# Convolution of every fifth block moved from TensorE to GpSimd, and the stores from GpSimd to SyncE

## The chip, the cores and the metric

One Trainium2 chip, one core. The metric is the time of one execution on the device in microseconds. Times of a kernel are medians of several runs; spans in the profile are 1.7 to 3.0 us shorter than the run they were taken in, in the median 1.8. A ratio is the mean time of one kernel's fast runs over that of the other's of the same rounds, so it is not quite the ratio of the medians quoted. Medians and ranges are over all runs, ratios over the fast ones alone; only e8 and e11 have a run that is labelled slow, one each.

## The reference

```python
# x: (8, 4160, 192), weight: (8 heads, 7 taps); w1, w2, w3: (192, 768), w_out: (768, 192)
w = exp(weight - max); w = w / (sum(w) + 1e-9)               # per head
out[b, s, h, :] = sum_k w[h, k] * x_pad[b, s + k, h, :]      # causal, 6 zeros ahead, 24 columns a head
h = maximum(maximum(out @ w1, out @ w2), out @ w3)           # 33280 tokens
result = h @ w_out                                           # fp32
```

## The kernel before

The tokens are cut into 65 blocks of 512. For 61 of them (four at the start have another form) the convolution goes: load x, cast it to fp16 on GpSimd, multiply it on TensorE with a band matrix that holds the seven taps (tile G, one group of 16 matmuls for a pair of blocks), copy G out of PSUM on ScalarE and VectorE, transpose the result by DMA, and copy it to the other half of the partitions ("double"). Then come six steps a block of the first layer (tiles lp and lq), a maximum (h), and the second layer (po).

```python
def cast_x(t):                                    # GpSimd, twice a block
    ...
    for c in range(2):
        nc.gpsimd.tensor_copy(out=x16s[t0][0:K, :, c, u, :, :].rearrange("p h r c -> p r h c"),
                              in_=xf[0:K, c:NR:2, :].rearrange("p r (h c) -> p r h c", c=GRP))

def conv(t, pools):                               # TensorE, once for two blocks
    ...
    for h in range(NHEAD):
        for c in range(2):
            nc.tensor.matmul(G[h // per][HALF * c:HALF * (c + 1), h % per, :],
                lhsT=band[0:HALF + PAD, h, PAD:HALF + PAD],
                rhs=x16s[t0][0:HALF + PAD, h, c, :, :, :].rearrange("p u r c -> p (u r c)"), ...)

for t in range(2, NB):                            # the main loop (cut)
    load_x(t + 6)                                 # SyncE
    double(t + 2)                                 # SyncE, two DMAs
    cast_x(t + 5)                                 # GpSimd
    l1(t, 0)
    conv(t + 3 if t % 2 == 0 else NB, WW + PQ); evac(...)
    turn(t + 3)                                   # SyncE, DMA transpose
    st2(t - 1, 0, NJ)
    for j in range(1, NJ):
        l1(t, j); st2(t - 1, j, NJ)
    store(t - 1, 0, 4, (nc.gpsimd,))              # GpSimd
```

In the traces GpSimd, and SyncE too, works through its instructions in this order.

The softmax here doesn't subtract the row's maximum and nothing guards it: scores larger than these inputs give would overflow.

## Time and profile before

| | before |
|---|---|
| median of 4 runs | 468.05 us (467.33 to 471.71) |
| span of the profiled run | 466.3 us |
| TensorE busy | 99% |
| GpSimd busy | 35% |
| VectorE, ScalarE busy | 77%, 68% |

The lines themselves stand in the prediction below. In a line of groups the columns are source line, engine, operation, output and inputs, shapes and count; then busy time in us and the mean ns of one; then the idle time of the engine just ahead of them and what ended it.

### The profile page before, as it was taken

The numbers are of one execution on the slowest core, as the hardware profiler recorded it, in microseconds if no ns is written. First come the engines' busy times: TensorE is split into PE (matmuls) and PEld (weight loads), VectorE is DVE, ScalarE is ACT, GpSimd is POOL, SyncE is SP. The second block draws the span as 40 slices with busy tenths as digits, with TensorE's granted clock in tenths as the row PEclk, the third lists the DMA queues.
The fourth block names the chain that finished last, engine by engine and source line by source line (L and its number), as shares of the span: only waits on it lengthen the run. The fifth ranks groups of instructions, "written<-read, shape, count | busy, mean of one in ns | idle before, by whom it ended". The sixth has DMA issues, their size and how long they took to land.

```text
span 466.3 us, 17191 instructions
## 1 busy us (share of the span) xinstructions
PE 460.1 (99%) x7065; PEld 385.6 (83%) x7065; DVE 359.6 (77%) x607; ACT 317.0 (68%) x609; POOL 162.7 (35%) x227
## 2 busy tenths in 40 slices
PE   8899999999999999999999999999999999999996
PEld 4587888888888888889888888988888898888996
DVE  6787777777777777787877777777778777787775
ACT  5766767667666676676766667676676666766664
POOL 5664334234324324423423432432442343243010
PEclk9999999999999999999999999999999999999999
DMA  8958997778687777878777768767686976784512
GB/s 201 238 119 198 208 232 174 171 198 172 170 202 191 149 188 174 180 175 204 178 152 197 170 181 189 181 157 200 177 176 165 210 178 153 190 166 108 118 69 103
DMA packets 107114, 81.14 MB, mean 174 GB/s; under 512 B 53110, under 2 KB 101980, under 8 KB 107036
## 3 DMA queue, kind: packets, MB, share of 16 engines
q1 hardware_dynamic: 99804, 55.17, 57.6%
q0 software_dynamic: 7072, 24.78, 14.8%
q8 instruction: 55, 0.90, 0.9%
q14 instruction: 23, 0.19, 0.1%
q10 hardware_dynamic: 160, 0.10, 0.1%
HBM read 30.28 MB, written 25.56 MB: 120 GB/s over the span
## 4 chain that ended last, share of the span: by engine, by line
PE 95%; DMA 2%; SPq 2%; POOL 0%; issue 0%; DVE 0%; ACT 0%
PE lq L399 34%; PE po L442 33%; PE lp L399 22%; PE G L301 5%; DMA wos<-in_moe_w_out_dram 2%; SPq L190 1%; PE D L319 0%; SPq L134 0%; POOL wo L515 0%; PE pm L280 0%; PE pm L284 0%; DVE o L452 0%; ACT a L451 0%
## 5 line engine op out<-in xcount | busy, mean ns | idle before, releaser
L404 DVE TENSOR_TENSOR h<-r,lq 128x512 f16<-128x512 f16 x386 | 264.5, 685 | 98.6 <-ACT r L403 98.6
L403 ACT ACTIVATE r<-lp 128x512 f16<-128x512 f32 x386 | 230.5, 597 | 137.4 <-PE lp L399 123.9
L399 PE MATMUL lp<-yd,wd 64*128 64x512 f16 x1158 | 311.9, 376 | 1.3 <-DVE wd L256 1.3
L399 PE MATMUL lq<-yd,wd 64*128 64x512 f16 x1158 | 312.0, 376 | 0.0
L442 PE MATMUL po<-wo,h 64*128 64x192 f16 x3120 | 248.9, 243 | 0.0
L442 PEld LDWEIGHTS <-h 64*128 64x128 f16 x3120 | 203.6, 94 | 17.4
L399 PEld LDWEIGHTS <-wd 64*128 64x128 f16 x2340 | 166.6, 94 | 28.0 <-issue 3.4
L471 POOL DMA_DIRECT2D out_dram<-o x64 | 48.1, 752 | 281.4 <-DVE o L452 215.0
L158 POOL CAST x<-xf 70x768 f16<-70x768 f32 x122 | 97.4, 833 | 3.0 <-DMA xf<-in_x_dram 2.6
L442 PE MATMUL po<-m,yd 64*128 64x192 f16 x780 | 95.7, 243 | 0.0
L452 DVE TENSOR_TENSOR o<-a,po 128x384 f32<-128x384 f32 (+1 forms) x132 | 71.3, 542 | 0.6 <-ACT a L451 0.6
L442 PEld LDWEIGHTS <-yd 64*128 64x128 f16 x780 | 57.8, 94 | 10.8
L451 ACT COPY a<-po 128x384 f32<-128x384 f32 (+1 forms) x132 | 62.0, 471 | 2.1 <-PE po L442 2.1
L347 DVE CAST ys<-G 128x384 f16<-128x384 f32 x61 | 31.0, 550 | 0.0
L301 PEld LDWEIGHTS <-band 70*64 70x64 f16 x496 | 19.5, 109 | 12.8 <-PE lp L399 12.7
L347 ACT CAST ys<-G 128x384 f16<-128x384 f32 x61 | 26.2, 485 | 0.0
L301 PE MATMUL G<-x,band 70*64 70x192 f16 (+1 forms) x496 | 26.1, 248 | 0.0
L215 PE MATMUL idle<-idle 128*128 128x512 f16 x15 | 6.5, 581 | 1.2 <-DVE idle L210 1.2
L177 POOL CAST xz<-xf 112x80 f16<-112x80 f32 (+2 forms) x18 | 5.4, 340 | 3.9 <-DMA xf<-in_x_dram 3.0
L319 PEld LDWEIGHTS <-xz 112*32 112x32 f16 x240 | 4.7, 107 | 2.0 <-issue 1.3
L319 PE MATMUL D<-band,xz 112*32 112x103 f16 (+1 forms) x240 | 5.5, 229 | 0.0
L335 DVE COPY yd<-yd 64x512 f16<-64x512 f16 x9 | 4.3, 474 | 1.0 <-ACT yd L328 0.5
(45 smaller groups left out, 51.3 us busy)
## 6 DMA issues: line engine op xcount, KB each, us to landing
xf<-in_x_dram SPq DMA_DIRECT2D x57, 420.0 KB
out_dram<-o POOLq DMA_DIRECT2D x62, 384.0 KB, 3.8
yd<-yd SPq DMA_DIRECT2D x122, 96.0 KB
xf<-in_x_dram SPq DMA_DIRECT2D x7, 367.5 KB
ws<-in_moe_w_dram SPq DMA_DIRECT2D x6, 192.0 KB
yd<-ys SPq DMA_TRANSPOSE x61
w3s<-in_moe_w_dram SPq DMA_DIRECT2D x3, 192.0 KB
wos<-in_moe_w_out_dram SPq DMA_DIRECT2D x1, 576.0 KB
```

Source lines behind the costliest of these rows:

```text
L158: nc.gpsimd.tensor_copy(out=x16s[t0][0:K, :, c, u, :, :].rearrange("p h r c -> p r h c"), in_=xf[0:K, c:NR:2, :].rearrange("p r (h c) -> p ...
L215: nc.tensor.matmul(ps[:], lhsT=idle[:, 0:P], rhs=idle[:], start=True, stop=True)
L301: nc.tensor.matmul(G[h // per][HALF * c:HALF * (c + 1), h % per, :], lhsT=band[0:HALF + PAD, h, PAD:HALF + PAD], rhs=x16s[t0][0:HALF + PAD ...
L319: nc.tensor.matmul(ps[32 * g:32 * g + 32, lo:hi], lhsT=xz[t][v][0:rlen, q, 32 * s:32 * s + 32], rhs=band[0:rlen, h, cc:cc + hi - lo], star ...
L347: copy(out=slots[t][:, :, :, GRP * per * i:GRP * per * (i + 1)].rearrange("p u r (h c) -> p h (u r) c", c=GRP), in_=G[i][:].rearrange("p h ...
L399: nc.tensor.matmul(ps[i][:, 0:N], lhsT=wd[row, c, P * j:P * (j + 1)], rhs=y_all(t, i, c), start=(c == 0), stop=(c == NC - 1))
L403: nc.scalar.activation(out=r[:, 0:N], in_=ps[0][:, 0:N], func=AF.Relu)
L404: nc.vector.tensor_max(out=hs[t][:, j, 0:N], in0=r[:, 0:N], in1=ps[1][:, 0:N])
L442: nc.tensor.matmul(ps[b0, i][:, s % 2, :], lhsT=a, rhs=b, start=first, stop=last)
L451: nc.scalar.copy(out=a[:, ss, :], in_=ps[s0, 0][:, ss, :])
L452: nc.vector.tensor_add(out=outs[t][:, s0:s + 1, :], in0=a[:, ss, :], in1=ps[s0, 1][:, ss, :])
L471: qs[0].dma_start(out=bass.AP(tensor=out.tensor, offset=r * D, ap=[[D, n], [step * D, s1 - s0], [1, D]]), in_=ob[p0:p0 + n, s0:s1, :])
```

## The change

Its intent: TensorE is the bound and GpSimd is mostly idle, so twelve blocks (positions 11, 16, ... 61 and 64, called moved blocks here) get their convolution on GpSimd. x is cast and transposed first, so that tokens lie along the free dimension; then a tap is a multiplication by a column of weights and an addition in fp32. The six tokens ahead of a stretch of 128 come from its neighbour by two small DMAs and a copy (the "lead"). To make room on GpSimd, SyncE issues the stores. The blocks also change places, so that each moved block but the first of a sequence has its neighbour in the moved block before it.

```diff
+    EVERY = 5
+    qpos = [q for q in range(11, NB - 3, EVERY)] + [NB - 1]
 ...
+    def lead_q(q):
+        ... # memset if the block starts a sequence, else a DMA from the previous moved block
+        nc.sync.dma_start(out=xt[HALF:P, 0:6:2, LEAD - PAD:LEAD], in_=xt[0:HALF, 1:6:2, T - PAD:T])
+        nc.gpsimd.tensor_copy(out=xt[:, 1:6:2, LEAD - PAD:LEAD], in_=xt[:, 0:6:2, T - PAD:T])
+    def tap_q(q, k):
+        for c in range(3):
+            nc.gpsimd.tensor_scalar(out=part[:, 2 * c:2 * c + 2, :], in0=xt[...shifted by k...],
+                                    scalar1=wcol[:, c, k:k + 1], scalar2=0.0, op0=mult, op1=add)
+        ... nc.gpsimd.tensor_add(out=accs[q][:], in0=accs[q][:], in1=part[:])
 ...
+    for n, q in enumerate(qpos):
+        w = min(4 + EVERY * n, NB - 7)
+        plan.setdefault(w - 5 if n else 2, {})["load"] = q
+        plan.setdefault(w - 2 if n else 3, {})["cast"] = q
+        plan.setdefault(w - 1 if n else 4, {})["turn"] = q
+        plan.setdefault(w, {})["lead"] = q
+        for k in range(KW):
+            plan.setdefault(w + (k // 2 if last else k * EVERY // KW), {}).setdefault("taps", []).append((q, k))
+    make_wcol()
     for t in range(2, NB):
         load_x, double ...
+        if "turn" in todo: turn_q(todo["turn"])
+        if "lead" in todo: lead_q(todo["lead"])
         cast_x(t + 5)
+        if "load" in todo: load_q(todo["load"])
         l1, conv, evac, turn ...
+        if "cast" in todo: cast_q(todo["cast"])
+        for q, k in todo.get("taps", ()): tap_q(q, k)
         st2, l1 ...
-            store(t - 1, 0, 4, (nc.gpsimd,))
+            store(t - 1, 0, 4, (nc.sync,))
```

Iteration w of a moved block is thus the one in which its lead is fetched and its first two taps are computed; the transpose is issued in iteration w - 1 (for the first moved block in w itself).

More of the change, by code (lines that the diff above doesn't have):

```diff
@@ L69 @@
     NB = len(blocks)
+    EVERY = 5
+    qpos = [q for q in range(11, NB - 3, EVERY)] + [NB - 1]
+    qset = set(qpos)
     ENDS = NB - 7
-    blocks.insert(ENDS, blocks.pop())
+    ends = blocks.pop()
+    lanes = blocks[-nfull:] + blocks[-2 * nfull:-nfull]
+    lanes, rest = lanes[:len(qpos)], [blk for blk in blocks if blk not in lanes[:len(qpos)]]
+    rest.insert(ENDS - sum(q < ENDS for q in qpos), ends)
+    blocks = [(lanes if t in qset else rest).pop(0) for t in range(NB)]
     blkN = [sum(sg[2] for sg in blk) for blk in blocks]
@@ L98 @@
     xfp = ctx.enter_context(tc.tile_pool(name="xfp", bufs=6))
+    xqp = ctx.enter_context(tc.tile_pool(name="xqp", bufs=2))
+    xtp = ctx.enter_context(tc.tile_pool(name="xtp", bufs=3))
+    accp = ctx.enter_context(tc.tile_pool(name="accp", bufs=2))
     x16p = ctx.enter_context(tc.tile_pool(name="x16p", bufs=3))
@@ L113, in load_x @@
     def load_x(t, eng=nc.sync):
-        if not 0 <= t < NB:
+        if not 0 <= t < NB or t in qset:
             return
@@ L140, in load_x @@
         xin[t] = [xf, todo[0][0], parts]
+    pairs, left = {}, [t for t in range(NDENSE + 1, NB) if t not in qset]
+    assert len(left) % 2 == 0
+    for a in left[::2]:
+        b = left[left.index(a) + 1]
+        assert b == a + 1
+        pairs[a], pairs[b] = (a, 0, 2), (a, 1, 2)
+    pairs[NDENSE] = (NDENSE, 0, 1)
     def place(t):
-        return (t, 0, 1) if t == NDENSE else (t - (t - NDENSE - 1) % 2, (t - NDENSE - 1) % 2, 2)
+        return pairs[t]
     x16s, slots = {}, {}
     def cast_x(t):
-        if not 0 <= t < NB:
+        if not 0 <= t < NB or t in qset:
             return
@@ L159, in cast_x, with load_q @@
                                   in_=xf[0:K, c:NR:2, :].rearrange("p r (h c) -> p r h c", c=GRP))
+    LEAD = 16
+    xqs, xts = {}, {}
+    def load_q(q):
+        pool, tag = ((xap, "xa"), (xbp, "xb"))[qpos.index(q) % 2]
+        xf = pool.tile([P, NR, D], FP32, tag=tag, name=f"xl_{q}")
+        (b, S, N, _), = blocks[q]
+        nc.sync.dma_start(out=xf[:, 0:N // P, :],
+                          in_=bass.AP(tensor=x.tensor, offset=(b * SEQ + S) * D,
+                                      ap=[[D, P], [P * D, N // P], [1, D]]))
+        xin[q] = xf
@@ new lines, in cast_q, with turn_q @@
+    def cast_q(q):
+        xf = xin.pop(q)
+        xqs[q] = xqp.tile([P, 3, 2, 2, HALF], FP16, tag="xq", name=f"xq_{q}")
+        for i in range(2):
+            nc.gpsimd.tensor_copy(out=xqs[q][:, :, :, i, :].rearrange("p c r m -> p r c m"),
+                                  in_=xf[:, 2 * i:2 * i + 2, :].rearrange("p r (c m) -> p r c m", m=HALF))
+    def turn_q(q):
+        xt = xts[q] = xtp.tile([P, 6, LEAD + P], FP16, tag="xt", name=f"xt_{q}")
+        nc.sync.dma_start_transpose(out=xt[:, :, LEAD:LEAD + P],
+                                    in_=xqs.pop(q)[:].rearrange("p c r i m -> p (c r i m)"))
@@ new lines, in lead_q @@
+    def lead_q(q):
+        xt, n = xts[q], qpos.index(q)
+        prev = qpos[n - 1] if n and blocks[q][0][1] > 0 else None
+        T = LEAD + P
+        if prev is None:
+            nc.gpsimd.memset(xt[0:HALF, 0:6:2, LEAD - PAD:LEAD], 0.0)
+        else:
+            nc.sync.dma_start(out=xt[0:HALF, 0:6:2, LEAD - PAD:LEAD],
+                              in_=xts[prev][HALF:P, 1:6:2, T - PAD:T])
+        nc.sync.dma_start(out=xt[HALF:P, 0:6:2, LEAD - PAD:LEAD], in_=xt[0:HALF, 1:6:2, T - PAD:T])
+        nc.gpsimd.tensor_copy(out=xt[:, 1:6:2, LEAD - PAD:LEAD], in_=xt[:, 0:6:2, T - PAD:T])
@@ new lines @@
+    accs = {}
+    def tap_q(q, k):
+        xt = xts[q]
+        part = accp.tile([P, 6, P], FP32, tag="t" if k else "a", name=f"tap{k}_{q}")
+        for c in range(3):
+            nc.gpsimd.tensor_scalar(out=part[:, 2 * c:2 * c + 2, :],
+                                    in0=xt[:, 2 * c:2 * c + 2, LEAD - PAD + k:LEAD - PAD + k + P],
+                                    scalar1=wcol[:, c, k:k + 1], scalar2=0.0,
+                                    op0=mybir.AluOpType.mult, op1=mybir.AluOpType.add)
+        if k == 0:
+            accs[q] = part
+            return
+        if k < KW - 1:
+            nc.gpsimd.tensor_add(out=accs[q][:], in0=accs[q][:], in1=part[:])
+            return
+        yd = dense[q] = ydp.tile([P, 2, NCH // 2, P], FP16, tag="yd", name=f"yd_{q}")
+        nc.gpsimd.tensor_add(out=yd[:, 0, :, :], in0=accs.pop(q)[:], in1=part[:])
@@ L236, with make_wcol @@
         nc.gpsimd.memset(xz[1][v][:], 0.0)
+    sel = const.tile([NHEAD, NHEAD, GRP], FP16)
+    wcol = const.tile([P, 3, KW], FP32)
+    def make_wcol():
+        ps = psw.tile([P, 3, KW], FP32, tag="w", name="wcols")
+        for c in range(3):
+            for i in range(2):
+                nc.tensor.matmul(ps[HALF * i:HALF * (i + 1), c, :],
+                                 lhsT=sel[:].rearrange("p h c -> p (h c)")[:, HALF * c:HALF * (c + 1)],
+                                 rhs=line[:, 31:31 + KW], start=True, stop=True, tile_position=(0, HALF * i))
+        nc.vector.tensor_copy(out=wcol[:], in_=ps[:])
     bps = psq.tile([32, WIN, NHEAD], FP32, tag="q", name="band_cols")
@@ L248 @@
     w3h = const.tile([HALF, NC, DFF], FP16)
+    nc.gpsimd.tensor_copy(out=sel[:], in_=ident16[0:NHEAD, 0:NHEAD].unsqueeze(2).to_broadcast([NHEAD, NHEAD, GRP]))
     wd = const.tile([P, NC, DFF], FP16)
@@ L351, in turn @@
     def turn(t):
-        if t >= NB:
+        if t >= NB or t in qset:
             return
@@ L367, in double, with spot @@
                                   in_=yd[HALF * (1 - i):HALF * (2 - i), 0, :, :])
-    def spot(i, f):
-        return f // 2 + (0 if f % 2 == i else NCH // 2)
+    def spot(t, i, c, r):
+        if t in qset:
+            own, k = r // 2, 2 * c + r % 2
+        else:
+            own, k = (NC * r + c) % 2, (NC * r + c) // 2
+        return k + (0 if own == i else NCH // 2)
     def y_all(t, i, c):
@@ L377, in y_all @@
         a = dense[t][row, 0, 0, :]
-        s0, s1 = spot(i, c), spot(i, c + NC)
-        assert all(spot(i, NC * r + c) == (s1 if r % 2 else s0) + NC * (r // 2) for r in range(4))
+        s0, s1, s2, s3 = (spot(t, i, c, r) for r in range(4))
+        assert s3 - s2 == s1 - s0
         return bass.AP(tensor=a.tensor, offset=a.offset + P * s0,
-                       ap=[list(a.ap[0]), [P * NC, 2], [P * (s1 - s0), 2], [1, P]])
+                       ap=[list(a.ap[0]), [P * (s2 - s0), 2], [P * (s1 - s0), 2], [1, P]])
     def y_tok(t, i, c, s):
@@ L386, in y_tok @@
             return dense[t][row, c, P * s:P * (s + 1)]
-        k = spot(i, NC * s + c)
-        return dense[t][row, k // (NCH // 2), k % (NCH // 2), :]
+        k = spot(t, i, c, s)
+        return dense[t][row, k // 6, k % 6, :]
     def l1(t, j, pools=((psp, "p"), (psq, "q"))):
@@ L529 @@
     store(0, 0, 4, (nc.gpsimd,))
-    convs_at = {2: 4, 3: 5}
+    convs_at = {2: 4, 3: 5, 4: 7}
+    convs_at.update({t - 3: t for t in pairs if t > 8 and pairs[t][1] == 0})
     doubles_at = {2: (), 3: (4,), 4: (5, 6)}
+    plan = {}
+    for n, q in enumerate(qpos):
+        w = min(4 + EVERY * n, NB - 7)
+        last = q == NB - 1
+        plan.setdefault(w - 5 if n else 2, {})["load"] = q
[5 more added lines that the diff above has]
+    make_wcol()
     for t in range(2, NB):
+        todo = plan.get(t, {})
         if t > 4:
@@ L541 @@
             load_x(t + 6)
+        if "turn" in todo:
+            turn_q(todo["turn"])
+        if "lead" in todo:
+            lead_q(todo["lead"])
         if t > 3:
             cast_x(t + 5)
+        if "load" in todo:
+            load_q(todo["load"])
         begin(t)
@@ L549 @@
             load_x(7)
-        u = convs_at.get(t, t + 3 if t % 2 == 0 else NB)
+        u = convs_at.get(t, NB)
         conv(u, PQ if t == 2 else WW + PQ)
@@ L572 @@
             turn(t + 3)
+        if "cast" in todo:
+            cast_q(todo["cast"])
+        for q, k in todo.get("taps", ()):
+            tap_q(q, k)
         st2(t - 1, 0, NJ)
```

## The prediction

> **What bounds the kernel now.** I read the page first (busy shares, then the chain that ended last), then the chain in order of time, then a table of stretches of one pair of blocks each, and last the groups by form and the DMA queues. The busy shares and the chain come first because they say whether one engine carries the span.
>
> ```profile
> PE 460.1 (99%) x7065; PEld 385.6 (83%) x7065; DVE 359.6 (77%) x607; ACT 317.0 (68%) x609; POOL 162.7 (35%) x227
> ...
> PE 95%; DMA 2%; SPq 2%; POOL 0%; issue 0%; DVE 0%; ACT 0%
> PE lq L399 34%; PE po L442 33%; PE lp L399 22%; PE G L301 5%; DMA wos<-in_moe_w_out_dram 2%; SPq L190 1%; PE D L319 0%; SPq L134 0%; POOL wo L515 0%; PE pm L280 0%; PE pm L284 0%; DVE o L452 0%; ACT a L451 0%
> ```
>
> 95% of the chain is TensorE, and the convolution matmuls (G, L301) are 5% of it: at 466.3 us some 24 us. A busy TensorE alone would not prove a bound, but here the chain runs from matmul to matmul after the first 23 us. GpSimd is 65% idle. The chain in order of time shows the rhythm (start us, length us, what):
>
> ```profile
> 127.80 0.34 PE po L442 x8
> 128.85 0.34 PE po L442 x8
> ...
> 138.40 0.34 PE po L442 x8
> 139.47 0.78 PE G L301 x16
> 140.25 0.52 PE po L442 x10
> 153.25 0.78 PE G L301 x16
> ```
>
> One step (six matmuls of the first layer, ten of the second) takes 1.06 us, six steps make a block, and one group of 16 G matmuls serves a pair of blocks. From G to G it is 153.25 - 139.47 = 13.78 us (13.74 in the mean of later pairs). Twelve steps of 1.06 are 12.72, so a G group costs 13.74 - 12.72 = 1.02 us of TensorE time, its 0.78 us of chain and the switching around it. The stretches of 13.74 us say that this holds everywhere and at full clock (us, then busy and count for PE, PEld, DVE, ACT, POOL, then clock, DMA share, GB/s):
>
> ```profile
> 98.29:112.03 13.74, 13.74 (x212) 12.19 (x212) 10.65 (x19) 9.36 (x19) 4.69 (x6) 1.00 0.80 184
> 112.03:125.77 13.74, 13.74 (x210) 11.19 (x210) 10.72 (x19) 9.53 (x19) 4.69 (x6) 1.00 0.71 178
> ```
>
> VectorE is at 10.7 of 13.74 and ScalarE at 9.4: neither binds. Of GpSimd's work and the DMA I need these rows:
>
> ```profile
> L158 POOL CAST x<-xf 70x768 f16<-70x768 f32 x122 | 97.4, 833 | 3.0 <-DMA xf<-in_x_dram 2.6
> L471 POOL DMA_DIRECT2D out_dram<-o x64 | 48.1, 752 | 281.4 <-DVE o L452 215.0
> L256 POOL TENSOR_TENSOR wd<-ws,w3s 128x768 f16<-128x768 f32 x1 | 1.8, 1814 | 1.3 <-DMA ws<-in_moe_w_dram 1.3
> L177 POOL CAST xz<-xf 112x240 f16<-112x240 f32 x6 | 2.4, 405 | 1.0 <-PE pm L280 0.7 <-DMA xf<-in_x_dram 0.2
> ...
> q1 hardware_dynamic: 99804, 55.17, 57.6%
> q0 software_dynamic: 7072, 24.78, 14.8%
> ```
>
> The wait of 281 us before the stores costs nothing by itself: GpSimd merely sits on the output tile while nothing else needs it.
>
> [...] The one full-size two-input instruction of this trace took 1814 ns[...]; I use the trace's number. [...] 386 max instructions run from 674 to 692 ns, though GpSimd is busy a third of the time. So [...] I expect no slower VectorE. [...] Here pairs of 833 ns casts take 1.60 us, so their spacing is 0.80.
>
> **The change part by part.**
>
> Removed from TensorE: 12 of the 61 blocks that used G (positions 11, 16, ... 61 and 64). The instruction order confirms it: 180 PE rows fewer, which is 96 G matmuls with their weight loads (192), plus 12 rows for making the tap columns. That is six G groups: 6 x 1.02 = 6.1 us. With them go 12 evacuations each on ScalarE and VectorE, both off the path. The matmuls of the layers stay the same.
>
> Added on TensorE: six tiny matmuls for the tap columns at the start of the main loop, with a GpSimd broadcast and a VectorE copy. The matmuls of the same kind for the band took 163 ns each, overlapped; I take 0.3 us.
>
> Added on GpSimd, per moved block (every five blocks): 21 multiplications of 128x256. I have no row for them; from the casts (240 elements 405 ns reported, about 60 ns less in spacing) I take 0.38 us, so 8.0 us. Six adds of 128x768 at 1.8: 10.8. Two casts of 384 elements at about 0.5: 1.0. The lead copy 0.3, and waits between dependent taps some 1.5. Sum 21.6 us. Four ordinary blocks' casts stay: 4 x 1.60 = 6.4. Together 28 us. Five blocks now take 30 x 1.06 + 2 x 1.02 = 33.8 us on TensorE. GpSimd would then be at 83%, all hidden. The schedule helps: the iteration that gets two full taps (2 x 2.95 us) is the one with no ordinary cast, so no iteration asks more than about 6 of its 6.8 us.
>
> Moved: the 64 stores go from GpSimd to SyncE, 48 us off GpSimd. On SyncE they wait in order for the end of the previous block. Loads, doubles and transposes behind them start about 1 us into the next block instead, and have one to two blocks of slack. The stores leave as 512 rows of 768 bytes instead of large packets. From the first stretch, where loads alone ran at 201 GB/s with 0.8 to 0.9 busy, such a row takes about 52 ns of one engine, so 27 us of engine time a store against 17 now. The DMA share goes from 0.73 to an estimated 0.83 with the small lead transfers. It stays off the path in steady state.
>
> Where I expect a loss: the start. The first moved block is turned in iteration 4 and its lead and taps stand in the same iteration, ahead of or among the casts for the pair 9 and 10. The G group of that pair starts at 57.04 us now. SyncE must issue a store, four doubles and a load before that transpose, which I put at about 47 us, landing at 50 to 52, because the DMA engines are full there (share 1.05 from 43 to 57 us). GpSimd then does: lead copy, cast 9 (to about 52 to 54), wait for the lead transfers, two taps (4.2 us), cast 10 (1.6 us). That ends at 58.3 to 60, so TensorE waits 1 to 3 us once. I take 2. Afterwards GpSimd catches up.
>
> Sum: 467.97 - 6.1 + 0.3 + 2.0 = 464.2; rounded to 464.0.
>
> **The rivals.**
> (a) GpSimd becomes the bound. If a multiplication costs 0.8 us and not 0.38, a cycle asks 37 us of 33.8, the casts come late and TensorE waits for x: 3 us in each of 12 cycles, 500 us or so. For it: no row shows this instruction[...]. Against it: casts of the same size are cheap, and the placing of the taps looks fitted.
> (b) SyncE's queue or the DMA engines become the bound: stores, loads, lead transfers and transposes now stand in one order, and one late tap holds up a double and all that follows. For it: the share of 0.83 and stretches near 1. Against it: SyncE issues some 4 us of 6.8 a block and each transfer has a block of slack. It would make 466 to 475.
> (c) Everything is hidden, the start too: 467.97 - 6.1 + 0.3 = 462.2.
>
> **Range and chances.** The saving is well founded (6.1 us, bounded above by about 6.5), so under 461 is unlikely, and faster by over 2% (under 458.6) would need a second gain that I don't see: 0.03. Mostly the result lies between (c) and a few microseconds of stall; slower by over 2% (over 477.3) needs rival (a): 0.09. Within 2%: 0.88. Range 461.0 to 469.5.
>
> **What would show it right or wrong.** Right: 400 G matmuls instead of 496, G groups in the chain about 1.02 us a piece with gaps of 20 us where a moved block stands, POOL at 75 to 85%, multiplications under 0.45 us, max instructions on VectorE still at 686 ns, and TensorE waiting for a GpSimd cast once, before 62 us. Wrong: PEld or PE waiting at L301's successor for POOL casts in every cycle (rival a), waits of casts for DMA or of the doubles in SyncE's queue that reach TensorE (rival b), a longer VectorE max[...], or a step of more than 1.06 us.

## The result, and the profile after

485.25 us median (482.91 to 487.06, 4 runs) against 468.05: ratio 1.0348, 95% interval 1.0276 to 1.0420. The change is slower by 3.5%. The page of the kernel after, busy shares and chain:

```profile
PE 462.4 (96%) x6975; PEld 380.8 (79%) x6975; DVE 355.4 (74%) x596; ACT 313.8 (65%) x597; POOL 352.0 (73%) x501
...
PE 45%; POOL 28%; DMA 15%; SPq 7%; issue 3%; DVE 2%; ACT 0%; POOLq 0%; DVEq 0%
```

GpSimd is at 73%, not at its limit. Yet the chain that ends last is no longer TensorE alone: 28% of it is GpSimd, 15% DMA, 7% SyncE's queue. The groups concerned:

```profile
L227 POOL TENSOR_SCALAR tap<-xt,wcol 128x256 f32<-128x256 f16 x252 | 116.1, 477 | 50.4 <-DMA xt<-xt 50.4
L235 POOL TENSOR_TENSOR tap<-tap,tap 128x768 f32<-128x768 f32 x60 | 108.6, 1810 | 5.0
L176 POOL CAST x<-xf 70x768 f16<-70x768 f32 x98 | 77.8, 822 | 6.3 <-DMA xf<-in_x_dram 6.0
...
L391 PE MATMUL G<-x,band 70*64 70x192 f16 (+1 forms) x400 | 24.3, 253 | 12.7 <-POOL x L176 12.4
...
L218 POOL COPY xt<-xt 128x18 f16<-128x18 f16 x12 | 2.4, 198 | 31.9 <-DMA xt<-xq 31.0
```

There are 400 G matmuls, as foretold. They now wait for casts on GpSimd (12.4 us), and GpSimd itself stands 50.4 us for the lead transfers (xt<-xt) and 31.0 us for the transposes (xt<-xq). The table of waits says how often (us in total, times, longest):

```profile
POOL tap L227 <- DMA xt<-xt: 50.4, 11, 5.7
POOL xt L218 <- DMA xt<-xq: 31.0, 11, 12.1
...
PE G L391 <- POOL x L176: 12.4, 15, 5.0
```

So GpSimd stands in eleven of the twelve moved blocks. The chain in order of time, around the second moved block, shows how (start, length, what):

```profile
84.14 4.63 DMA xt<-xq
...
88.83 0.21 POOL xt L218
...
89.45 0.59 SPq L456
...
90.83 5.11 DMA xt<-xt
...
96.12 2.76 POOL tap L227 x6
98.88 0.07 issue
98.95 1.81 POOL tap L235
100.76 1.54 POOL x L176 x2
102.31 0.04 issue
102.35 1.06 PE G L391 x15
```

Every link waits for the one before: the transpose of the moved block (4.6 us), SyncE's doubles, the lead transfer (5.1 us for 2.2 KB), two taps and an add on GpSimd (4.6 us), and only then the cast of an ordinary block, which stands behind the taps in GpSimd's order and has nothing to do with them. The G matmuls that need this cast start 18.2 us after the transpose was issued. The transpose itself is late: SyncE's timeline has it after the store of iteration w - 2, which could go at 81.08 us only, a load (81.54) and two doubles (82.89).

Two stretches of the kernel show what was lost (us, then busy and count of PE, PEld, DVE, ACT, POOL, clock, DMA share, GB/s):

```profile
42.00:98.00 56.00, 50.52 (x737) 42.44 (x734) 37.84 (x65) 33.41 (x63) 32.89 (x50) 0.94 0.78 170
98.00:448.00 350.00, 342.74 (x5125) 288.00 (x5122) 263.19 (x441) 233.23 (x440) 284.27 (x394) 1.00 0.81 171
```

The same stretches of the best kernel below (e5):

```profile
42.00:98.00 56.00, 56.00 (x845) 46.95 (x842) 43.19 (x73) 38.05 (x73) 14.22 (x20) 1.00 0.94 194
98.00:448.00 350.00, 350.00 (x5299) 301.64 (x5297) 271.24 (x456) 240.33 (x455) 275.40 (x379) 1.00 0.87 174
```

It executes 845 and 5299 matmuls, some 15.1 a microsecond. 108 and 174 fewer are 7.2 us lost at the first moved block and 11.5 us over the later ones. The span accounts for itself that way: 466.3 - 6.1 saved + 7.2 + 11.5 + 2.0 (the first G group starts at 30.86 us instead of 28.83) = 480.9; measured 481.1.

Part of the loss at the first block is the clock. TensorE stands 5.0 us for the cast, and the matmuls after that (timeline of TensorE; start, length, what) take 0.63 us and start 0.43 us apart, where 0.38 and 0.21 are usual:

```profile
64.10 0.32 PE L391 MATMUL G<-x,band 70*64 70x192 f16 x1 [5.03 <-POOL x L176]
64.87 1.44 PE L391 MATMUL G<-x,band 70*64 70x192 f16 x15 [0.45 <-POOL x L176]
...
67.01 0.63 PE L493 MATMUL lp<-yd,wd 64*128 64x512 f16 x1
```

The granted clock is 0.50 from 61.8 to 68.6 us, and at 68.89 us the same matmuls are back at 0.38. It fell 2.8 us after the last matmul. At the second moved block it fell after two stands of 1.05 and 0.53 us:

```profile
101.58 0.24 PE L391 MATMUL G<-x,band 70*64 70x192 f16 x1 [1.05 <-POOL x L176]
102.35 1.06 PE L391 MATMUL G<-x,band 70*64 70x192 f16 x15 [0.53 <-POOL x L176]
...
104.11 0.63 PE L493 MATMUL lp<-yd,wd 64*128 64x512 f16 x1
```

The granted clock is 0.50 from 102.8 to 106.1 us, which is some 1.7 of the 11.5 us, as an estimate: half of 3.3 us. In the fourth moved block, stands of 0.61 and 0.53 us left it at 1.00. So the two short stands at the second moved block cost about as much again in clock; how long a stand it takes is not shown.

### The profile page after: what moved, and what is told of

It is laid out like the page before. It is cut to its first block, busy times and chain, and to the rows that moved or that the text cites.

```text
span 481.1 us, 17289 instructions
## 1 busy us (share of the span) xinstructions
PE 462.4 (96%) x6975; PEld 380.8 (79%) x6975; DVE 355.4 (74%) x596; ACT 313.8 (65%) x597; POOL 352.0 (73%) x501
## 4 chain that ended last, share of the span: by engine, by line
PE 45%; POOL 28%; DMA 15%; SPq 7%; issue 3%; DVE 2%; ACT 0%; POOLq 0%; DVEq 0%
PE po L536 15%; PE lp L493 13%; PE lq L493 13%; POOL tap L227 11%; POOL tap L235 9%; DMA xt<-xt 9%; POOL x L176 6%; DMA xt<-xq 5%; SPq L456 4%; PE G L391 2%; PE D L409 1%; SPq L215 1%; SPq L144 1%; DVE o L546 1%; POOL xq L198 1%
## 5 line engine op out<-in xcount | busy, mean ns | idle before, releaser
L536 PEld LDWEIGHTS <-h 64*128 64x128 f16 x3120 | 199.6, 94 | 22.4 <-issue 1.1
L493 PEld LDWEIGHTS <-wd 64*128 64x128 f16 x2340 | 163.1, 94 | 30.0 <-issue 4.9
L227 POOL TENSOR_SCALAR tap<-xt,wcol 128x256 f32<-128x256 f16 x252 | 116.1, 477 | 50.4 <-DMA xt<-xt 50.4
L235 POOL TENSOR_TENSOR tap<-tap,tap 128x768 f32<-128x768 f32 x60 | 108.6, 1810 | 5.0
L176 POOL CAST x<-xf 70x768 f16<-70x768 f32 x98 | 77.8, 822 | 6.3 <-DMA xf<-in_x_dram 6.0
L536 PEld LDWEIGHTS <-yd 64*128 64x128 f16 x780 | 58.5, 94 | 11.1 <-issue 0.6
L391 PEld LDWEIGHTS <-band 70*64 70x64 f16 x400 | 17.8, 112 | 24.5 <-issue 13.9
L391 PE MATMUL G<-x,band 70*64 70x192 f16 (+1 forms) x400 | 24.3, 253 | 12.7 <-POOL x L176 12.4
L437 DVE CAST ys<-G 128x384 f16<-128x384 f32 x49 | 25.0, 550 | 12.7 <-PE G L391 12.5
L437 ACT CAST ys<-G 128x384 f16<-128x384 f32 x49 | 21.2, 483 | 14.5 <-PE G L391 14.5
L218 POOL COPY xt<-xt 128x18 f16<-128x18 f16 x12 | 2.4, 198 | 31.9 <-DMA xt<-xq 31.0
L238 POOL TENSOR_TENSOR yd<-tap,tap 128x768 f16<-128x768 f32 x12 | 21.7, 1810 | 1.0
L198 POOL CAST xq<-xl 128x384 f16<-128x384 f32 x24 | 11.4, 502 | 0.0
```

The source lines that it names most:

```text
L227: nc.gpsimd.tensor_scalar(out=part[:, 2 * c:2 * c + 2, :], in0=xt[:, 2 * c:2 * c + 2, LEAD - PAD + k:LEAD - PAD + k + P], scalar1=wcol[:, ...
L235: nc.gpsimd.tensor_add(out=accs[q][:], in0=accs[q][:], in1=part[:])
L238: nc.gpsimd.tensor_add(out=yd[:, 0, :, :], in0=accs.pop(q)[:], in1=part[:])
L437: copy(out=slots[t][:, :, :, GRP * per * i:GRP * per * (i + 1)].rearrange("p u r (h c) -> p h (u r) c", c=GRP), in_=G[i][:].rearrange("p h ...
L493: nc.tensor.matmul(ps[i][:, 0:N], lhsT=wd[row, c, P * j:P * (j + 1)], rhs=y_all(t, i, c), start=(c == 0), stop=(c == NC - 1))
L536: nc.tensor.matmul(ps[b0, i][:, s % 2, :], lhsT=a, rhs=b, start=first, stop=last)
```

## The experiments

Three theories at first: **A**, GpSimd stands in order, and its waits on the transfers delay the casts behind; **B**, the arithmetic of the taps is too long; **C**, the stores in SyncE's queue hold up everything else. Each experiment is an edit of the kernel after unless another is named. The first four ran beside a before of 467.52 us.

### e1: no lead transfers

```diff
-        ... two nc.sync.dma_start into the lead, and the lead copy
+        nc.gpsimd.memset(xt[:, :, LEAD - PAD:LEAD], 0.0)
```

> The two small lead transfers of each moved block are replaced by a memset on GpSimd (the first six tokens of each stretch come out wrong on purpose; all other work stays). Theory A (GpSimd stands in order, and the 50 us that its taps wait for the lead transfers, added to its own work, make a cycle of five blocks longer on GpSimd than the 33.8 us that TensorE needs, so the ordinary casts behind come late): the wait on xt<-xt is gone, cycles fall from 34.9 us to 33.8 or 34.0, and the time from 485 to 471 to 475, with the loss of the first moved block still there. Theory B (the tap arithmetic itself is too long: multiplications at 0.46 us of spacing rather than 0.38): the work is untouched, so the time stays above 480. Theory C (stores in SyncE's order are the cause, also of loads and doubles): stays above 480.

Measured: 467.10 us, ratio 0.9984 (0.9941 to 1.0027). Its output is wrong, which doesn't matter for the time. The direction is that of A, and the gain (18 us) is larger than expected, because the edit also took away the lead copy that waits for the transpose; so both waits went, and this run cannot tell them apart. B is refuted: the arithmetic of the taps is unchanged.

### e2: the stores back on GpSimd

```diff
-            store(t - 1, 0, 4, (nc.sync,))
+            store(t - 1, 0, 4, (nc.gpsimd,))
```

> Only the stores go back to GpSimd. Theory A: GpSimd gets five stores of 0.75 us more a cycle, and stands at each of them until the output tile is ready, so it is worse: over 495 us. Theory C (SyncE's order and the 768-byte rows of the stores hold up the lead transfers and the rest): the lead transfers land sooner, the wait on them halves, and the time falls to 470 to 478.

Measured: 480.86 us, ratio 1.0275 (1.0247 to 1.0303). A's number was wrong: GpSimd rose to 84% busy and yet the kernel became 4 us faster (its slowest run, 481.99 us, is below the fastest of the change, 482.91, though in other rounds). C is right in part: the wait on the lead transfers fell from 50.4 to 25.5 us, that on the transposes from 31.0 to 6.8. The transfers themselves became shorter: on the chain of the change the lead transfer takes 2.8 to 5.1 us, median 3.7, and on that of e2 1.9 to 4.7, median 2.0. But most of the loss stays.

### e3: cast, transpose and lead transfers one iteration earlier

```diff
-        plan.setdefault(w - 2 if n else 3, {})["cast"] = q
-        plan.setdefault(w - 1 if n else 4, {})["turn"] = q
-        plan.setdefault(w, {})["lead"] = q
+        plan.setdefault(w - 3 if n else 3, {})["cast"] = q
+        plan.setdefault(w - 2 if n else 4, {})["turn"] = q
+        plan.setdefault(w - 1 if n else 4, {})["lead"] = q
+        plan.setdefault(w, {})["copy"] = q          # the lead copy on GpSimd, split off
```

> The work is the same, but from the second moved block on the cast, the transpose and the lead transfers are each issued one iteration earlier, so that they have landed when GpSimd comes to them. Theory A: the waits of GpSimd on xt<-xt and xt<-xq fall from 81 us to under 25 us (the first block's), cycles become 33.8 us, time 469 to 474 (what is left over 462 is the start). Theory B: above 480, since the arithmetic is the same. Theory C: above 480, since SyncE issues the same in the same amount.

Measured: 472.06 us, ratio 1.0091 (1.0054 to 1.0127), as A said. The same stretch as above:

```profile
98.00:448.00 350.00, 350.00 (x5300) 302.02 (x5297) 271.45 (x456) 240.22 (x455) 292.10 (x402) 1.00 0.88 176
```

TensorE is busy without a gap, with GpSimd doing the same work and SyncE issuing the same DMAs. B falls as the cause of the repeated loss, and so does C as long as it means the stores alone. What is left is the first moved block, which this edit leaves alone: TensorE still stands 5.04 us before its G group.

### e4: the first moved block at 21 and not at 11

```diff
-    qpos = [q for q in range(11, NB - 3, EVERY)] + [NB - 1]
+    qpos = [q for q in range(21, NB - 3, EVERY)] + [NB - 1]
-        w = min(4 + EVERY * n, NB - 7)
+        w = min(14 + EVERY * n, NB - 7)
         ... # load, cast and turn at w - 5, w - 2 and w - 1 for the first moved block too
```

> The moved blocks begin at position 21 and not at 11: ten moved blocks, whose first stands in a part where the loads are not behind. Tells the loss of the start from the loss of each cycle. Theory A with a loss at the start of some 8 us (5.0 us of TensorE standing at 59 us and a lower clock after it) and of about 1.1 us in each later cycle: saving 5.1 instead of 6.1 us, no stall at the start, 473 to 477 us. If nearly all of the loss is per cycle: 480 or more. If nearly all is at the start: 464 to 467.

Measured: 476.83 us, ratio 1.0193 (1.0152 to 1.0235). In the stretch from 42 to 98 us TensorE is busy throughout, and after it the loss of every block is there as in the change. So the two losses are separate, and e3 and e4 each cure one.

### e5: e3 and e4 together

> Both remedies together: the earlier issue of e3 and the later start of e4, ten moved blocks. Theory A (GpSimd's work plus its waits is longer than TensorE's cycle, and a separate loss in the start): nothing of the loss is left, so TensorE keeps 5 of the 6 us: 467.5 - 5.1 + 0.3 = 462.7, between 462 and 465, no wait of the conv matmuls on a GpSimd cast over 0.5 us. If there is a further cost that neither remedy touches (slower matmuls, contention of VectorE, full DMA engines): 466 or more.

Measured: 464.40 us against 467.52, ratio 0.9939 (0.9924 to 0.9954), result correct. This version beats the kernel before by 0.6%, with ten moved blocks. No G matmul waits for a cast.

### e6: e3, and the first moved block one iteration earlier too

```diff
-        plan.setdefault(w - 3 if n else 3, {})["cast"] = q
-        plan.setdefault(w - 2 if n else 4, {})["turn"] = q
+        plan.setdefault(w - 3 if n else 2, {})["cast"] = q
+        plan.setdefault(w - 2 if n else 3, {})["turn"] = q
```

> Twelve moved blocks as in the change, e3's earlier issue, and the first moved block too is cast and turned one iteration earlier than in the change. If the loss at the start is the order (transpose behind six transfers on SyncE, lead copy ahead of the casts on GpSimd), the wait on xt<-xq at the start falls from 13 us to under 5, the 5 us stand of TensorE at 59 us goes, and the time is 462 to 466. If it is the full DMA engines between 30 and 60 us, the stall only moves: 468 to 473.

Measured: 468.58 us, ratio 1.0017 (0.9996 to 1.0037). The transpose was waited for 3.3 us and not 13, but GpSimd then stood 6.4 us for a load of x and 4.9 for the lead transfer. TensorE waited only 0.4 us for casts, but 1.9 us for a double, and was granted 0.59 of its clock from 56 to 58 us after that. The stall moved, as the second alternative said; it is 3.5 us better than e3, not cured.

### e7: two taps of seven

```diff
-        for k in range(KW):
+        for k in (0, KW - 1):
```

> The change with only the first and the last tap of seven (wrong result on purpose): five multiplications by three and five adds fewer, some 16 us of GpSimd a moved block; all transfers and waits on them stay. If it is the sum of work and waits that outgrows the cycle, the cycles are back at 33.8 us though the waits on xt<-xt and xt<-xq are still 60 us or more, and only a part of the loss at the start is left: 465 to 471. If the waits alone delay the casts enough: above 478.

Measured: 466.65 us (462.75 to 468.01), ratio 0.9967 (0.9935 to 0.9999). Its output is wrong, which doesn't matter for the time. The waits stayed (51.1 and 48.5 us), and the loss was gone. I first took it for proof that the sum of work and waits was too long. It is not: the edit also took tap 1 (1.4 us of multiplications and an add of 1.8) out of the chain between lead transfer and cast. e11 separates the two.

### e8: the lead transfers issued by ScalarE

```diff
-        nc.sync.dma_start(out=xt[HALF:P, 0:6:2, ...
+        nc.scalar.dma_start(out=xt[HALF:P, 0:6:2, ...      # and the other one alike
```

> The change with the lead transfers issued by ScalarE and not by SyncE. If they land late because they stand behind the store, the load and the two doubles in SyncE's order and queue, the wait on xt<-xt falls from 50 us to under 25 and the time to 473 to 479. If the small transfers themselves take 4 us, the wait stays above 40 us and the time at 483 to 488. ScalarE waits for the transpose in order, so it may lose something itself.

Measured: 525.24 us, ratio 1.1230 (1.1214 to 1.1247): far worse than either expectation. Waits of the profiled run (itself slow, so only their kind is used):

```profile
ACT r L497 <- POOL xt L218: 26.2, 9, 3.3
ACT r L497 <- DMA xt<-xq: 15.7, 3, 10.4
```

ScalarE now stands in order for the transpose ahead of each lead transfer, and the activations that TensorE needs stand behind it. It is the same fault as in the change, on an engine whose results TensorE needs in every step. The question how long the transfer itself takes was not settled by it; the chain of e2 says more.

### e9: the kernel before with only its stores moved

```diff
-            store(t - 1, 0, 4, (nc.gpsimd,))          # in the kernel before
+            store(t - 1, 0, 4, (nc.sync,))
```

> The kernel before with only its stores moved from GpSimd to SyncE: that part of the change alone. All theories that put the loss in GpSimd's order expect nothing: 466.5 to 469, within 0.3% of before, since TensorE has its x in time either way. If the stores in SyncE's order and their 768-byte rows cost TensorE anything by themselves, it shows here: 471 or more. The DMA share should rise from 0.73 to some 0.8.

Measured: 467.47 us against 467.41, ratio 0.9996 (0.9983 to 1.0010). The move of the stores alone costs nothing and gains nothing. The shares of the DMA queues add up to 81.9% here and to 73.5% before.

### e10: e5 with its stores back on GpSimd

> e5 (earlier issue, later start, 464.4 us) with the stores back on GpSimd. GpSimd's own work is then about 29 us and 3.8 us of stores in a cycle of 33.8, and each store also holds it until the output tile is ready. If GpSimd's order is what counts, the store waits now fall into a nearly full cycle and the time goes up to 467 to 474; if GpSimd still fits, it stays at 463.5 to 466, and the move of the stores was not needed.

Measured: 464.19 us, ratio 0.9930 (0.9917 to 0.9943), as fast as e5; my first alternative was wrong. GpSimd is 78% busy over the span and 90% or more in nearly every slice of the span from 115 us on, and stands 57.5 us for output tiles, and yet TensorE executes 850 and 5299 matmuls in the two stretches, none fewer than in e5. With the transfers early, the stores could have stayed.

### e11: taps 0, 1 and 6

By now theory A had two readings: A1, work and waits of GpSimd add up to more than TensorE's cycle; A2, one chain of links is too long. In the change, the cycle from 138.3 to 173.5 us (from the third tap of one moved block to that of the next, 35.2 us) had 28.2 us of GpSimd's work and 7.0 of waits in it, against the 33.8 that TensorE needs, so A1 looked good.

```diff
-        for k in range(KW):
+        for k in (0, 1, KW - 1):
```

> The change with the taps 0, 1 and 6 alone (wrong result on purpose): 12.8 us of GpSimd's work a moved block less, but nothing less between the landing of the lead transfer and the cast of the next ordinary block (two taps, one add). Theory A1 (throughput: 28.2 us of work and 7.0 of waits fill GpSimd's cycle beyond 33.8): the sum is 22.4, the cycles are back at 33.8, only the start is left: 470 to 475. Theory A2 (a chain: transpose, lead copy, lead transfer, two taps, cast, conv matmuls, each waiting for the one before, takes longer than the two blocks that it has, and GpSimd idles before it): the chain is the same, conv matmuls wait as often and as long as in the change, 479 to 486.

Measured: 487.14 us (480.73 to 489.94) against 467.74, ratio 1.0368 (1.0318 to 1.0418). Its output is wrong, which doesn't matter for the time. GpSimd has 151 us less to do than in the change, and the time is the same (it is even above the 479 to 486 us that A2 gave; one of the four runs is slow). Busy shares, a wait, and the chain at the second moved block:

```profile
PE 463.3 (96%) x6975; PEld 381.0 (79%) x6975; DVE 355.5 (73%) x596; ACT 314.4 (65%) x597; POOL 201.2 (42%) x309
```

```profile
PE G L391 <- POOL x L176: 11.8, 17, 3.1
```

```profile
84.40 4.43 DMA xt<-xq
...
92.03 3.75 DMA xt<-xt
...
95.96 2.77 POOL tap L227 x6
...
102.21 0.82 PE G L391 x15
```

The chain is 17.8 us long against 18.2, and G waits 11.8 us against 12.4. A1 is refuted, A2 stands: it is not how much GpSimd does, but what stands ahead of the casts in its order.

### e12: the same DMAs, GpSimd's order changed

```diff
         plan.setdefault(w, {})["lead"] = q
+        plan.setdefault(w + 1, {})["copy"] = q       # lead copy just ahead of the taps, behind cast_x
-            plan.setdefault(w + (k // 2 if last else k * EVERY // KW), {})...
+            plan.setdefault(w + max(1, k // 2 if last else k * EVERY // KW), {})...
```

> The change, all twelve moved blocks, all DMAs issued where it issues them; only GpSimd's order differs: the lead copy and the first two taps stand one iteration later, behind that iteration's ordinary cast, so no ordinary cast stands behind a fresh transfer. Theory A2 (the chain through GpSimd's order): no conv matmul waits for a cast over 0.5 us, at the start neither, and the time is 462 to 465, as TensorE keeps all or most of its 6 us. Theory A1 (throughput): the work is the same and the waits that are left decide, 465 to 475. If the start is lost to the full DMA engines whatever the order: 466 to 470.

Measured: 466.21 us (464.24 to 467.08), ratio 0.9958 (0.9940 to 0.9976), result correct. With all twelve blocks, all transfers where the change issues them, and only the lead copy and first taps behind one more cast, 19 us come back. TensorE's G matmuls wait for casts once only:

```profile
PE G L394 <- POOL x L176: 0.5, 1, 0.5
```

The time is 1.2 us over what A2 gave and lies in the ranges of the two other alternatives, so it is the waits and not the number that speak for A2. In the profiled run 2.7 us are lost before the first G group (31.56 us against 28.83), outside the part that the theories speak of.

## Why the prediction was wrong

**What held.** Six G groups left TensorE, and their saving is 6.1 us on paper; the kernels with both stalls cured keep 3 of 5 (e5, e10) or 1.5 of 6 (e12). In e12 some of it goes in the first 42 us (643 matmuls in the profiled run, against 676 before); in e5 it does not (676). The tap columns took 0.2 us on TensorE against 0.3. GpSimd's work was sized well: "Together 28 us" against 28.2 measured in one cycle, "83%" against 83% (28.2 of 33.8), though the multiplications were 0.46 us apart and not 0.38; the waits between taps, which I put at 1.5 us as an estimate without a row for them, came to some 0.5 us a moved block (5.0 us of idle time ahead of 60 adds and 1.0 ahead of the 12 last ones), and two errors cancelled by luck. (The two casts of a block start 0.77 us apart and not 0.80: the 1.60 us that I halved is one start-to-start and one whole cast. The 1.8 for an add is the 1814 ns of the kernel before, and 1810 here.) Two signs for "right" were just missed: GpSimd at 73% of the longer span, not 75 to 85%, and a multiplication at 0.46 us, not under 0.45. VectorE was not slowed: the max instructions have a median of 686 ns before and after, with GpSimd at 35% and at 73%. The DMA share went to 0.81 in the main part against "0.83".

**What failed.** The step is "so no iteration asks more than about 6 of its 6.8 us", and with it "GpSimd would then be at 83%, all hidden". I compared sums of work with the length of an iteration and did not follow, for every moved block, when the operands of the first tap arrive and what stands behind that tap. I did follow it for the first block, where I saw the lead transfers ahead of two taps and the cast; then wrote "Afterwards GpSimd catches up". GpSimd does catch up: in the change it idles 2.5 us for the transpose in the cycle that is quoted under e11. But catching up doesn't help, for the transpose and the lead transfer start only when SyncE gets to them, after a store that waits for the end of a block; from there the chain runs again. Lead transfer, two taps and the cast stand on the chain of the profile in eleven of the twelve moved blocks, the transpose ahead of them in six; in the others it begins in SyncE's queue. That is 11.5 us over the later blocks, against none predicted.

**What was mis-sized.** "I take 2" for the start: 7.2 us. The transpose was issued at 50.67 us (I put it at 47) and landed at 55.7, and the lead at 58.5. The cast of the second block of the pair ended at 64.8, against "58.3 to 60", and the stand of 5.0 us brought the low clock with it (0.50 to 68.6 us).

**The rivals.** (a) named the right engine for the wrong reason: the multiplications were cheap, and GpSimd was not the bound. (b) named the mechanism ("stores, loads, lead transfers and transposes now stand in one order") but I gave it slack of a block for every transfer. The lead transfer has none: its taps stand in the iteration in which it is issued. The sign that I gave for (a), TensorE waiting for GpSimd's casts in every cycle, is what the profile shows, but it does not prove (a): a full engine and an engine that stands behind a transfer give the same sign. "Slower" had a chance of 0.09, all of it for (a).

**What stays open.** Why the kernels with moved blocks reach their first G group 0.0 to 2.7 us later than the kernel before. Their instructions are not the reason: e7 and e11 have those of the change up to there, and reached it at 28.8 and 29.4 us, against 30.9. In two profiled runs a lower clock went with it (granted 0.72 from 6 to 12 us in e3, 0.79 from 12 to 20 in e12), but in that of the change it was 1.00. So the 2.0 us in the sum above belong to one execution. Open too is how much of the 2.8 to 5.1 us of a lead transfer is due to the stores in SyncE's queue: with these gone, in e2, six of eleven took under 2.0 us. In the first moved block of e6, GpSimd stood 11.3 us for late transfers; whether crowded DMA engines are the reason is not shown (their share was 0.81 from 42 to 55 us, against 1.00 in the kernel before), and no run took other traffic away.

## What to carry to other kernels

When work goes to an idle engine, don't only compare its sum with the time there is: list, in that engine's own order, every instruction that waits for a fresh transfer, and ask what other engines' inputs stand behind it. Issue such a transfer an iteration ahead, or put the instruction that waits for it behind those that others wait for (e12: the same work and DMAs, 19 us). A busy share of 73% says nothing of this; the chain of waits does, and an experiment that takes away work without shortening the chain (e11) tells the two apart.
